# Attention and a SoLU layer on one core: the softmax scale moved into the turn of the exponentials, with another order of work and of loads

## The chip, the core and the metric

The kernel runs on one core of a Trainium2 chip. The metric is the device time of one execution in microseconds; lower is better. A kernel is timed in several runs, and one further execution is profiled. Five engines work side by side: TensorE (PE in the profile, its weight loads PEld), VectorE (DVE), ScalarE (ACT), GpSimd (POOL) and SyncE (SP), which here only issues loads.

## The reference

Local attention with block summaries, over 4 batches, 8 heads, 768 positions, head size 64; then a feed-forward layer with the SoLU activation. Cut to what matters:

```python
k_sum = k.reshape(B, H, nb, block, D).max(axis=3)       # 24 blocks of 32
v_sum = v.reshape(B, H, nb, block, D).mean(axis=3)
scores_l = where(|i - j| < 16, scale * q @ k.T, -1e9)
scores_s = scale * q @ k_sum.T + log(block)
a = exp(scores_all - max);  a = a / (sum(a) + 1e-9)     # over [scores_l, scores_s]
x = a @ concat(v, v_sum)                                # then (3072, 512)
h = x @ w_in                                            # (3072, 1024)
solu = h * softmax(h)
ln = (solu - mean) / sqrt(var + 1e-6) * g_ln
out = ln @ w_out                                        # (3072, 512)
```

All inputs are float32, q and k larger than the others by a factor of 8.

## The kernel before, in words

**Attention** goes in 24 steps `(b, g, pp)`: batch, a group of 4 tiles of 64 queries, and a half of the four head pairs. A step has 8 blocks of 128 rows (two tiles of 64 queries) by 120 columns: 96 neighbouring keys and 24 block maxima. `scores` gathers the keys into `kw`, multiplies on TensorE into `s` (a PSUM buffer), and on VectorE adds the mask and takes the row maximum into `nm` while it copies to `e` (L574). ScalarE takes the exponentials of `e` in place and their sums `z` (L582). VectorE takes 1 / `z` and multiplies `e` by it (`MUL_E`, listed by its helper at L265). `values_turn` turns the result: 16 transposes of 64x120 with the identity into `t` (a PSUM buffer, L610), copied to `at` in two halves by ScalarE (L258) or VectorE (L259). `values` multiplies `at` with the values `vt`, whose last 24 rows are the block means `vsum`, into `x` (L649), which is split into a high and a low part, `xh` and `xl`.

**The layer** goes in 24 tiles of 128 tokens, one for each attention step. `first(t)`: three products for each piece of w_in (high and low parts) into `h` (L674, 24 products of 512 columns), row maxima `hm`, exponentials `he`, the SoLU product, centring, squares, and a small chain on GpSimd for the inverse root `y`. `turn(t)`: 16 transposes into `lt`, split into `lh` and `ll`. `second(t)`: 24 products with w_out into `o` (L752), scaled by `y` and stored from ScalarE's queue.

**Weights.** w_in and w_out come as 64-bit words in 16 pieces of 512 KB (`raw`). For each piece `rounded` and `split_w_in` or `split_w_out` do eight operations on VectorE, ScalarE or GpSimd (`cv`, then `w`): w_in's eight pieces before the first `h`, w_out's two at a time in the first four tiles.

**Block means.** For batch 0 and 1 they are products with a selector (`vs_ps<-st_v`), later a tree of additions on GpSimd (`st_v`, `vacc`, L478) and products with the identity (L493). `load_v2` writes `vsum` into `vt` by a DMA on ScalarE's queue (L518).

**What sets the order.** The program isn't issued as it is written. `Plan` collects operations, each with the engines that may run it, the planner's price there, and what it depends on. `issue` simulates the engines with those prices, always takes the operation that can begin first (ties by a due time that is the place of its TensorE user in the program), chooses the engine by price plus a surcharge (`DEAR`), and then issues everything in the simulated order, each engine's queue in strict order. `keep_up` puts products with a tile of zeros (`zero`, L877; "idle products" below) into gaps of the first 80 us that the simulation sees on TensorE. The first loads follow the string `LOADS`: k, q are keys and queries of the first step, w pieces of w_in, r value rows for the means, v and V the first two `vt`, Q the second group's queries. From tile `NEAR` = 6 on, the TensorE work of a step is tied into one run: `t`, `lt`, `x`, `s`, then `o` and `h`.

Of the kernel before, what the change touches and what calls it, by code (L numbers as in the profile page):

```python
# [10 lines left out]
F32 = mybir.dt.float32  # L11
# [21 lines left out]
KC = WIN + NB  # L33
# [7 lines left out]
MEANS = 2  # L41
DIRECT = 0
NEAR = 6
WPT = 2


LOADS = "kqkkqkwwwwwwwwrrrvQV"
NEG = -8.0e9
# [24 lines left out]
class Plan:  # L73
# [65 lines left out]
    def issue(self):  # L139
        ready, free, then, dma, held = {}, {}, {}, 0.0, 0.0  # L140
        for o in self.ops:
            o.left = len(o.deps)
            for d in o.deps:
                d.users.append(o)
        for o in reversed(self.ops):
            o.due = min([u.due for u in o.users] + ([o.prio] if "pe" in o.can else []), default=o.prio)
            if "sp" in o.can:
                o.due = o.prio

        def enter(o):  # L150
# [38 lines left out]
        order = []  # L189
        while len(order) < len(self.ops):  # L190
            t, e, o = min(((x[0], e, x[1]) for e in ready for x in [take(e)] if x),
                          key=lambda x: (x[0], x[2].due))
# [18 lines left out]
        at, done = self.START, set()  # L211
        for o in order:
            if o.engine == "pe":
                while at + self.SYNC < min(o.start, self.FILL):
                    at += self.keep_up(at, done)
                at = max(at, o.start) + o.cost * (2 if o.start < self.COLD else 1)
            done.add(o)
            o.fn()

# [12 lines left out]
def attn_then_solu(ctx: ExitStack, tc: tile.TileContext, q, k, v, vr, vb, w_in, w_out, g_ln, out):  # L232
# [3 lines left out]
    nc = tc.nc  # L236
    plan = Plan()
    op = plan.op
# [9 lines left out]
    ADD_W = ((dve, 0.62), (pool, 1.46))  # L248
    MUL_E = ((pool, 1.8), (dve, 1.07))

# [24 lines left out]
    g_sb = const.tile([P, NFC], F32, name="g_sb")  # L275
    zero = const.tile([P, 512], BF16, name="zero")

    make_identity(nc, ident)
    nc.gpsimd.memset(mhalf, -0.5)
    nc.vector.memset(zero, 0.0)  # L280
# [50 lines left out]
    def load_w(key, src, after=()):  # L331
        raw[key] = x = plan.buf(const, [P, 1024], I32, f"w{key}", 1, f"raw{key}")
        op(sp, 0.43, lambda: nc.sync.dma_start(out=x.ap, in_=src.bitcast(I32)), w=[x], nbytes=P * 4096,
           after=after)

    def rounded(key, tag, bufs):

# [4 lines left out]
        high, low = (lambda: st.ap[:, 0]), (lambda: st.ap[:, 1])  # L342


        op(act, 0.57, lambda: nc.scalar.activation(
            out=high().bitcast(F32), in_=words(1).bitcast(F32), func=AF.Copy, scale=2.0 ** -112),
            r=[x], w=[(st, 0)], alt=[(dve, 0.34, lambda: nc.vector.tensor_scalar(
                out=high().bitcast(F32), in0=words(1).bitcast(F32), scalar1=2.0 ** -112, scalar2=None,
                op0=ALU.mult))], port=True)

# [164 lines left out]
    def load_v2(b, g):  # L515
        x, y = vt[b, g], vsum[b]

        return op(act, 0.8, lambda: nc.scalar.dma_start(  # L518
            out=x.ap[WIN:KC], in_=y.ap[WIN:KC, :].rearrange("p (o c) -> p o c", o=1).broadcast_to([NB, G, DM])),
                  r=[y], w=[(x, 1)], nbytes=NB * 8192)  # L520

    def scores(b, g, pp, direct=False, each=False):
# [89 lines left out]
    def values_turn(b, g, pp):  # L612
        nm_ = f"{b}_{g}_{pp}"
        e = es.pop((b, g, pp))
# [200 lines left out]
    for t in range(NT):  # L815
# [3 lines left out]
        if not near:  # L819
            run(scores(*step(t + 2), t < DIRECT))  # L820

# [99 lines left out]
```

## Time and profile before

| | |
|---|---|
| median of three runs | 406.12 us (405.17 to 410.25) |
| the profiled execution's own time | 406.69 us |
| its span, first to last instruction | 404.9 us |
| TensorE busy | 388.3 us, 3702 matmul records |
| VectorE, ScalarE, GpSimd busy | 300.5, 230.5, 88.8 us |
| granted clock of TensorE, mean | 0.99 |
| read from HBM, written | 40.11 MB, 6.29 MB |

How to read the rows: a group row gives line, engine, operation, what is written from what, partitions by elements, count, then busy time in us and mean ns of one, then the engine's idle time just before such instructions and what ended most of it. A row of the timeline begins with its start and its length in us, from the span's start; a bracket at its end is the idle time before it and who ended it. Matmul records are pipelined, so what a group costs TensorE is the distance from its first start to the next group's first start, not the sum of its lengths. PEld is the load of the stationary operand, ACTq and SPq a queue's issue of a DMA.

### The profile page before, as it was taken

Reading aid. Unit: us, or ns where it says so; the run is one execution under the profiler, and the core shown is the slowest. Engines: PE = TensorE matmul, PEld = TensorE weight load, DVE = VectorE, ACT = ScalarE, POOL = GpSimd, SP = SyncE. Lnnn points to the kernel's source line nnn. Section 1 sums busy time; section 2 is a strip of 40 time slices with the busy share of each in tenths; the row PEclk is TensorE's granted clock in tenths of the full one; section 3 lists DMA queues with packets and bytes.
Section 4 is the critical chain, followed back from the end, with each engine's and each line's share of the span. In section 5 each row is a group of like instructions: output and inputs, shape, how many; then the busy total and the mean of one; then the engine's idle time right before and its main releaser. Section 6 shows DMA issues by size and latency. Waiting matters only on the chain.

```text
span 404.9 us, 9684 instructions
## 1 busy us (share of the span) xinstructions
PE 388.3 (96%) x3702; PEld 299.6 (74%) x3702; DVE 300.5 (74%) x933; ACT 230.5 (57%) x711; POOL 88.8 (22%) x231
## 2 busy tenths in 40 slices
PE   7999999986988999998999999999999999999996
PEld 3436667664876788887888888878878888888776
DVE  4998999989887886776877777687678766654430
ACT  2967788963898664565455664646545453423311
POOL 3020240305581412216202211201201221011100
PEclk9999999996999999999999999999999999999999
DMA  8999992044257040044350040141130000000011
GB/s 270 411 409 364 404 336 75 25 123 152 86 186 258 26 159 28 28 176 126 108 182 21 28 182 2 40 169 42 41 137 2 28 28 26 2 26 28 26 53 52
DMA packets 14994, 49.24 MB, mean 122 GB/s; under 512 B 1836, under 2 KB 2092, under 8 KB 13412
## 3 DMA queue, kind: packets, MB, share of 16 engines
q1 hardware_dynamic: 10112, 40.12, 27.4%
q10 hardware_dynamic: 4836, 8.51, 6.9%
q8 instruction: 29, 0.48, 0.5%
q14 instruction: 17, 0.14, 0.1%
HBM read 40.11 MB, written 6.29 MB: 115 GB/s over the span
## 4 chain that ended last, share of the span: by engine, by line
PE 71%; DMA 12%; DVE 11%; ACT 3%; issue 1%; POOL 1%; SPq 0%; ACTq 0%; POOLq 0%
PE o L752 32%; PE h L674 23%; PE x L649 5%; PE s L555 4%; DMA kraw<-in_k 3%; DMA qt<-in_q 3%; PE lt L610 3%; DMA raw<-in_w_in 2%; PE t L610 2%; DMA vt<-in_v 2%; DMA st_v<-in_vb 1%; DVE e L265 1%; DVE e L574 1%; DVE hm L684 1%; DVE ksum L416 1%
## 5 line engine op out<-in xcount | busy, mean ns | idle before, releaser
L752 PE MATMUL o<-w,lh 128*128 128x512 f32 (+1 forms) x400 | 129.6, 393 | 4.8 <-DVE w L379 4.8
L674 PE MATMUL h<-w,xh 128*128 128x512 f32 x384 | 125.6, 396 | 0.0
L582 ACT ACTIVATE e<-e,nm 128x120 f32<-128x120 f32 x192 | 73.1, 385 | 40.2 <-DVE nm L574 31.1
L752 PEld LDWEIGHTS o<-w,lh 128*128 128x128 f32 x400 | 74.6, 189 | 23.9 <-DVE w L379 5.6
L674 PEld LDWEIGHTS h<-w,xh 128*128 128x128 f32 x384 | 72.1, 188 | 17.4 <-DVE he L697 0.5
L752 PE MATMUL o<-w,ll 128*128 128x512 f32 (+1 forms) x200 | 77.3, 386 | 0.0
L674 PE MATMUL h<-w,xl 128*128 128x512 f32 x192 | 75.5, 393 | 0.0
L684 DVE TENSOR_REDUCE hm<-h 128x1 f32<-128x512 f32 x48 | 32.7, 684 | 33.8 <-PE h L674 33.5
L716 POOL TENSOR_SCALAR ss<-ss 128x1 f32<-128x1 f32 x24 | 6.4, 268 | 167.7 <-ACT sq L712 151.9
L752 PEld LDWEIGHTS o<-w,ll 128*128 128x128 f32 x200 | 38.0, 190 | 6.4
L674 PEld LDWEIGHTS h<-w,xl 128*128 128x128 f32 x192 | 36.1, 188 | 7.8 <-DVE xl L655 0.3
L574 DVE CUSTOM_DVE_ANT_0 e<-s,mask 128x120 f32<-128x120 f32 x192 | 40.6, 276 | 0.1
L689 ACT ACTIVATE he<-h,hm 128x512 f32<-128x512 f32 x48 | 32.8, 691 | 13.9 <-DVE hm L686 13.9
L258 ACT COPY at<-t 120x512 f32<-120x512 f32 x29 | 16.3, 585 | 35.6 <-PE t L610 35.1
L582 ACT ACTIVATION_READ_ACCUMULATOR e<-e,nm 128x1 f32 x192 | 36.4, 190 | 0.0
L697 DVE SCALAR_TENSOR_TENSOR he<-h,hz,he 128x512 f32<-128x512 f32 x48 | 34.2, 744 | 0.2
L737 DVE TENSOR_TENSOR ll<-lt,lh 128x512 fp32r<-128x512 f32 x48 | 31.6, 679 | 0.2
L649 PE MATMUL x<-at,vt 120*64 120x64 f32 (+1 forms) x768 | 28.3, 225 | 0.4 <-DVE at L259 0.4
L265 DVE TENSOR_TENSOR e<-e,z 128x960 f32<-128x960 f32 x24 | 28.5, 1189 | 0.1
L478 POOL TENSOR_TENSOR st_v<-st_v 96x512 f32<-96x512 f32 (+3 forms) x28 | 22.1, 791 | 29.2 <-DMA st_v<-in_vb 28.5
L649 PEld LDWEIGHTS x<-at,vt 120*64 120x64 f32 (+1 forms) x768 | 24.6, 138 | 5.2 <-issue 2.3
L712 ACT ACTIVATE sq<-he 128x1024 bf16<-128x1024 f32 x24 | 25.2, 1050 | 5.3 <-DVE hm L684 2.7
(93 smaller groups left out, 504.2 us busy)
## 6 DMA issues: line engine op xcount, KB each, us to landing
vt<-in_v SPq DMA_DIRECT2D x12, 1024.0 KB, 6.2
kraw<-in_k SPq DMA_DIRECT2D x16, 400.0 KB, 8.5
out<-os ACTq DMA_DIRECT2D x23, 256.0 KB, 2.1
qt<-in_q SPq DMA_DIRECT2D x11, 512.0 KB, 5.4
raw<-in_w_in SPq DMA_DIRECT2D x8, 512.0 KB, 10.1
raw<-in_w_out SPq DMA_DIRECT2D x8, 512.0 KB, 10.1
st_v<-in_vr SPq DMA_DIRECT2D x6, 512.0 KB
st_v<-in_vb SPq DMA_DIRECT2D x8, 384.0 KB, 3.4
```

The lines of the kernel that those rows point to most:

```text
L265: by = {dve: lambda: nc.vector.tensor_tensor(out=to(), in0=a(), in1=b(), op=kind), pool: lambda: nc.gpsimd.tensor_tensor(out=to(), in0=a() ...
L478: op(pool, 0.15 + w * 0.0021, lambda w=w, o=o: nc.gpsimd.tensor_tensor(out=o.ap[:n, :w], in0=x.ap[:n, :w], in1=x.ap[:n, w:2 * w], op=ALU.add),
L574: nc.vector.tensor_tensor_reduce(out=e.ap[:, n, :], in0=sc.ap[:, j, (2 * i + up) * KC:(2 * i + up + 1) * KC], in1=mask[:, mi, :], scale=-S ...
L582: nc.scalar.activation(out=e.ap[:, n, :], in_=e.ap[:, n, :], func=AF.Exp, bias=nm.ap[:, n:n + 1], scale=-1.0, accum_out=z.ap[:, n:n + 1])
L649: nc.tensor.matmul(xp()[j * D:(j + 1) * D, i, qs], vs.ap[:k, u, cs], at.ap[:k, u % 2, n[j] + u // 2, :], start=not apart, stop=not apart o ...
L674: nc.tensor.matmul(hp.ap, a.ap[:, c, ts], w.ap[:, i], start=(c == 0 and n == 0), stop=(c == NKC - 1 and n == 2))
L684: op(dve, 0.6, lambda i=i, hp=hp: nc.vector.tensor_reduce(out=nms.ap[:, i:i + 1], in_=hp.ap, op=ALU.max, axis=AX.X, negate=True), r=[hp], ...
L689: op(act, 0.71, lambda i=i, hp=hp: nc.scalar.activation(out=part(i), in_=hp.ap, func=AF.Exp, bias=nm.ap, accum_out=zs.ap[:, i:i + 1]), r=[ ...
L697: op(dve, 0.67, lambda i=i, hp=hp: nc.vector.scalar_tensor_tensor(out=part(i), in0=hp.ap, scalar=zs.ap[:, 0:1], in1=part(i), op0=ALU.mult, ...
L712: op(act, 1.13, lambda: nc.scalar.activation(out=sq.ap, in_=e.ap, func=AF.Square, accum_out=ss.ap), r=[e], w=[sq, ss])
L737: op(dve, 0.6, lambda part=part, r=r: nc.vector.tensor_tensor(out=part(lo), in0=tp.ap[:, r], in1=part(hi).bitcast(F32), op=ALU.subtract), ...
L752: nc.tensor.matmul(o.ap[:, cols], a.ap[:, f, :], w.ap[:, i, cols], start=(f == 0 and n == 0), stop=(f == NFC - 1 and n == 2))
```

## The change

1. The multiplication of the exponentials (128x960) goes. Instead `ident2`, two 64x64 identities one above the other, is multiplied by 1 / `z` into `dg` (128x512, `MUL_Z`): eight pairs of diagonal 64x64 blocks. `values_turn` multiplies `e` with these blocks by 16 ordinary float32 products where it had 16 transposes; the planner's price of the group stays 0.82.
2. `issue` tries 64 orders. In the first the due times are as before, in the others they carry noise (3.0 in standard deviation, in places of the program). Of the orders that come to an end, the one whose last TensorE operation ends first by the planner's prices is issued. The simulation itself moves to `order`.
3. Other prices: VectorE's surcharge is 1.0 for 0.6; a DMA behind 50 us is taken to land 2.0 us after its transfer, not 0.6.
4. The first loads come in another order; `load_v2` of batches 1 to 3 goes on SyncE's queue, of batch 0 stays on ScalarE's. `DIRECT`, which was 0, and `rebias`, a part of `rounded` with a name of its own, change nothing by themselves.

```diff
-LOADS = "kqkkqkwwwwwwwwrrrvQV"
+LOADS = "wkwqkkwkqwwrwrrwwvQV"
...
+    LATE = 50.0
...
-    DEAR = {"dve": 0.6, "act": 0.3, "pool": 1.0}
+    DEAR = {"dve": 1.0, "act": 0.3, "pool": 1.0}
+    TRIES, NOISE = 64, 3.0
...
+        due, best = [o.due for o in self.ops], None
+        for seed in range(self.TRIES):
+            noise = random.Random(seed)
+            for o, x in zip(self.ops, due):
+                o.due = x + (noise.gauss(0.0, self.NOISE) if seed else 0.0)
+            order = self.order()
+            if order:
+                end = max(o.end for o in order if "pe" in o.can)
+                if best is None or end < best[0]:
+                    best = end, order, [(o.start, o.end, o.engine, o.cost, o.fn) for o in self.ops]
...
-                o.end = dma + 0.6
+                o.end = dma + (0.6 if dma < self.LATE else 2.0)
...
-    MUL_E = ((pool, 1.8), (dve, 1.07))
+    MUL_Z = ((pool, 1.37), (dve, 0.6))
...
+    nc.gpsimd.tensor_tensor(out=ident2, in0=ident[:, :QT], in1=ident[:, QT:], op=ALU.add)
...
-        return op(act, 0.8, lambda: nc.scalar.dma_start(
+        e, cost, queue = (sp, 0.43, nc.sync) if b else (act, 0.8, nc.scalar)
+        return op(e, cost, lambda: queue.dma_start(
...
-        tt(MUL_E, ALU.mult, lambda: e.ap, lambda: e.ap,
-           lambda: z.ap.rearrange("p (u o) -> p u o", o=1).broadcast_to([P, 8, KC]), r=[z], w=[e], port=True)
-        es[b, g, pp] = e
+        dg = plan.buf(sb, [P, 8, QT], F32, "dg", 2, "dg" + nm_)
+        tt(MUL_Z, ALU.mult, lambda: dg.ap, lambda: ident2[:].rearrange("p (o q) -> p o q", o=1).broadcast_to([P, 8, QT]),
+           lambda: z.ap.rearrange("p (u o) -> p u o", o=1).broadcast_to([P, 8, QT]), r=[z], w=[dg], port=True)
+        es[b, g, pp] = e, dg
...
-        yield 0.82, lambda: turn_halves(tp.ap[:KC], lambda n: e.ap[:, n, :]), [e], [tp]
+        def mm():
+            for n in range(8):
+                for r in range(2):
+                    rows = slice(r * QT, (r + 1) * QT)
+                    nc.tensor.matmul(tp.ap[:KC, r, n, :], e.ap[rows, n, :], dg.ap[rows, n, :], start=True, stop=True)
+        yield 0.82, mm, [e, dg], [tp]
```

Counted over the whole order: VectorE loses 24 multiplications of `e`, 16 copies of `at`, 15 centrings of `he`, 7 scalings of `os` and 3 products of low parts of w_in, and gets 23 of `dg`; ScalarE gets the 16 copies, 7 scalings and 3 centrings and loses 9 issues of `vt<-vsum`; GpSimd gets 12 centrings, those 3 products and one `dg`; TensorE has 74 idle products for 82.

TensorE in the steady part, one period, before:

```order
L674 MATMUL h11_1_2751<-w7_546,xh1_2_2253 128x512
L610 MATMUL t2_1_0_2770<-ident_66,e2_1_0_2694 120x64 x16
L610 MATMUL lt8_2790<-ident_66,he8_2228 128x64 x16
L649 MATMUL x2_0_1_2807<-at2_0_1_2628,vt2_0_2066 64x64 x16
L555 MATMUL s2_1_1_2835<-kw2_1_1_2453,qt2_1_2077 64x120 x16
L752 MATMUL o7_2860<-w8_718,lh7_2660 128x512
```

and now:

```order
L711 MATMUL h11_1_2746<-w7_551,xh1_2_2262 128x512
L653 MATMUL t2_1_0_2780<-dg2_1_0_2763,e2_1_0_2702 120x64 x16
L641 MATMUL lt8_2800<-ident_66,he8_2235 128x64 x16
L686 MATMUL x2_0_1_2817<-at2_0_1_2639,vt2_0_2065 64x64 x16
L584 MATMUL s2_1_1_2844<-kw2_1_1_2461,qt2_1_2078 64x120 x16
L789 MATMUL o7_2870<-w8_723,lh7_2665 128x512
```

The sequence of the groups is the same; the first group's second operand is `dg` where it was the identity, its count the same.

ScalarE where w_out's last pieces (`w14`, `w15`; `raw15` is the last as it comes) are made ready, before:

```order
L377 ACTIVATE w13_1260<-cv13_1121,g_sb_69 128x512
L587 ACTIVATE z1_0_0_1179<-z1_0_0_1179 128x8
L258 CAST lh1_1262<-lt1_1212 128x8x64
L518 DMA vt1_1_1229<-vsum1_896 24x4x512
L345 ACTIVATE cv15_1280<-raw15_272 128x512
L377 ACTIVATE w14_1291<-cv14_1254,g_sb_69 128x512
```

and now:

```order
L380 ACTIVATE cv15_1266<-raw15_267 128x512
L611 ACTIVATE e1_0_0_1177,z1_0_0_1213<-e1_0_0_1177,nm1_0_0_1178 128x120 x4
L281 CAST lh1_1286<-lt1_1218 128x8x64
L616 ACTIVATE z1_0_0_1213<-z1_0_0_1213 128x8
L406 ACTIVATE w14_1299<-cv14_1251,g_sb_69 128x512
L406 ACTIVATE w15_1307<-cv15_1266,g_sb_69 128x512
```

The DMA `vt1_1<-vsum1` is gone from this queue (it stands on SyncE's now, behind the load of `vt1_1`), and the first operation on `raw15` stands earlier.

SyncE's loads from the first value rows (`st_v0_0`) to the two first `vt`, before:

```order
L424 DMA st_v0_0_153<-in_vr 128x1024
L424 DMA st_v0_1_158<-in_vr 128x1024
L424 DMA st_v0_2_160<-in_vr 128x1024
L512 DMA vt0_0_179<-in_v 128x2048
L506 DMA qt0_1_183<-in_q 128x1024
L512 DMA vt0_1_185<-in_v 128x2048
```

and now:

```order
L453 DMA st_v0_0_124<-in_vr 128x1024
L453 DMA st_v0_1_127<-in_vr 128x1024
L358 DMA raw6_131<-in_w_in 128x1024
L358 DMA raw7_133<-in_w_in 128x1024
L815 DMA g_sb_69<-in_g_ln 128x8
L535 DMA qt0_1_137<-in_q 128x1024
L453 DMA st_v0_2_143<-in_vr 128x1024
L541 DMA vt0_1_147<-in_v 128x2048
L541 DMA vt0_0_151<-in_v 128x2048
```

The first two `st_v` now stand ahead of w_in's last two pieces, the third behind them, and the two `vt` have changed places.

More of the change, by code (lines that the diff above doesn't have):

```diff
@@ L1 @@
 import math
+import random
 from contextlib import ExitStack
@@ L139, in issue @@
     def issue(self):
-        ready, free, then, dma, held = {}, {}, {}, 0.0, 0.0
         for o in self.ops:
-            o.left = len(o.deps)
             for d in o.deps:
@@ L148, in issue, with order @@
                 o.due = o.prio
+        due, best = [o.due for o in self.ops], None
[8 more added lines that the diff above has]
+                    best = end, order, [(o.start, o.end, o.engine, o.cost, o.fn) for o in self.ops]
+        _, order, kept = best
+        for o, x in zip(self.ops, kept):
+            o.start, o.end, o.engine, o.cost, o.fn = x
+        at, done = self.START, set()
+        for o in order:
+            if o.engine == "pe":
+                while at + self.SYNC < min(o.start, self.FILL):
+                    at += self.keep_up(at, done)
+                at = max(at, o.start) + o.cost * (2 if o.start < self.COLD else 1)
+            done.add(o)
+            o.fn()
+    def order(self):
+        ready, free, then, dma, held = {}, {}, {}, 0.0, 0.0
+        for o in self.ops:
+            o.left = len(o.deps)
         def enter(o):
@@ L191, in issue @@
             t, e, o = min(((x[0], e, x[1]) for e in ready for x in [take(e)] if x),
-                          key=lambda x: (x[0], x[2].due))
+                          key=lambda x: (x[0], x[2].due), default=(0.0, None, None))
+            if o is None:
+                return None
             for f in o.can:
@@ L210, in issue @@
                     enter(u)
[L211 to L218, printed above, removed]
+        return order
     def keep_up(self, at, done):
@@ L276, in attn_then_solu @@
     zero = const.tile([P, 512], BF16, name="zero")
+    ident2 = const.tile([P, QT], F32, name="ident2")
     make_identity(nc, ident)
+    nc.gpsimd.tensor_tensor(out=ident2, in0=ident[:, :QT], in1=ident[:, QT:], op=ALU.add)
     nc.gpsimd.memset(mhalf, -0.5)
@@ L334, in load_w, with rebias @@
            after=after)
+    def rebias(x, words, st, i):
+        to = lambda: st.ap[:, i].bitcast(F32)
+        op(act, 0.57, lambda: nc.scalar.activation(
+            out=to(), in_=words(1).bitcast(F32), func=AF.Copy, scale=2.0 ** -112),
+            r=[x], w=[(st, i)], alt=[(dve, 0.34, lambda: nc.vector.tensor_scalar(
+                out=to(), in0=words(1).bitcast(F32), scalar1=2.0 ** -112, scalar2=None,
+                op0=ALU.mult))], port=True)
     def rounded(key, tag, bufs):
@@ L342, in rounded @@
         high, low = (lambda: st.ap[:, 0]), (lambda: st.ap[:, 1])
[L345 to L349, printed above, removed]
+        rebias(x, words, st, 0)
         op(act, 0.57, lambda: nc.scalar.activation(
@@ L516, in load_v2 @@
         x, y = vt[b, g], vsum[b]
[L518 removed]
+        e, cost, queue = (sp, 0.43, nc.sync) if b else (act, 0.8, nc.scalar)
+        return op(e, cost, lambda: queue.dma_start(
             out=x.ap[WIN:KC], in_=y.ap[WIN:KC, :].rearrange("p (o c) -> p o c", o=1).broadcast_to([NB, G, DM])),
[L520 removed]
+            r=[y], w=[(x, 1)], nbytes=NB * 8192)
     def scores(b, g, pp, direct=False, each=False):
@@ L613, in values_turn @@
         nm_ = f"{b}_{g}_{pp}"
-        e = es.pop((b, g, pp))
+        e, dg = es.pop((b, g, pp))
         tp = plan.buf(ps, [P, 2, 8, QT], F32, "s", 2, f"t{nm_}")
-        yield 0.82, lambda: turn_halves(tp.ap[:KC], lambda n: e.ap[:, n, :]), [e], [tp]
+        def mm():
[4 more added lines that the diff above has]
+        yield 0.82, mm, [e, dg], [tp]
         at = plan.buf(sb, [P, 2, 8, QT], F32, "at", 2, f"at{nm_}")
@@ L819, in attn_then_solu @@
         if not near:
-            run(scores(*step(t + 2), t < DIRECT))
+            run(scores(*step(t + 2)))
         if t == NEAR - 1 or (near and j == 0 and n + 3 < len(its)):
```

1 line of the change is left out of this document (removed).

## The prediction

> **What bounds the kernel now.** I read the page's sums first, then busy time by stretch, then TensorE's own order of time inside the stretches, and last what the other engines did where TensorE waited.
>
> ```profile
> PE 388.3 (96%) x3702; PEld 299.6 (74%) x3702; DVE 300.5 (74%) x933; ACT 230.5 (57%) x711; POOL 88.8 (22%) x231
> PEclk9999999996999999999999999999999999999999
> ```
>
> TensorE is busy for 96% of the span, and its granted clock drops once, in the tenth slice. The stretches:
>
> ```profile
> core 0: us, PE busy (x) PEld busy (x) DVE busy (x) ACT busy (x) POOL busy (x), PEclk, DMA share, GB/s
> 0.00:36.30 36.30, 32.33 (x348) 15.36 (x348) 29.32 (x82) 23.53 (x62) 7.11 (x29) 1.00 0.96 368
> 36.30:87.80 51.50, 50.83 (x522) 36.62 (x519) 50.77 (x174) 42.68 (x139) 10.57 (x19) 1.00 0.60 212
> 87.80:101.50 13.70, 8.95 (x68) 6.01 (x67) 11.58 (x34) 4.75 (x7) 5.62 (x7) 0.75 0.44 129
> 101.50:141.70 40.20, 37.48 (x391) 29.92 (x389) 33.52 (x108) 32.66 (x108) 20.45 (x49) 1.00 0.41 139
> 141.70:333.70 192.00, 190.61 (x1936) 155.95 (x1935) 142.94 (x470) 105.87 (x354) 39.05 (x105) 1.00 0.25 80
> ```
>
> Three regimes. Up to 36.3 us the loads set the pace (DMA share 0.96). From 36.3 to 101.5 us VectorE has no room (50.77 of 51.50 us), and from 87.8 to 101.5 us TensorE waits for it: 8.95 of 13.70 us busy. From 141.7 us on TensorE is full, VectorE at 74%, ScalarE at 55%, so there every added microsecond of TensorE work lengthens the kernel, and VectorE time saved buys nothing. One period there, TensorE alone:
>
> ```profile
> 201.29 0.69 PE L610 MATMUL t<-ident,e 64*120 64x64 f32 x16
> 201.81 0.67 PE L610 MATMUL lt<-ident,he 64*128 64x64 f32 x16
> 202.41 1.15 PE L649 MATMUL x<-at,vt 120*64 120x64 f32 x32
> 203.49 1.05 PE L555 MATMUL s<-kw,qt 64*64 64x120 f32 x32
> 204.47 0.50 PE L752 MATMUL o<-w,lh 128*128 128x512 f32 x1
> ```
>
> What a group costs is the distance to the next group's start: `t` 0.52 us, `lt` 0.60, `x` 1.08, `s` 0.98. And the counts matter: the program issues 16 transposes for `t` and the trace has 16 records; it issues 16 float32 products for `x`, 16 for `s`, and the trace has 32 each. A float32 product is two passes here, a transpose is one.
>
> **The change, part by part.**
>
> *The products in place of the transposes.* The order shows 24 groups of 16 turn instructions, now `t<-dg,e` with the same shapes. They become float32 products, so 32 records. Price of a record: `x` has products with 64 moving columns, two at a time side by side, 1.08 us / 32 = 34 ns; the transposes, with the same 64x120 stationary tile, two halves of the rows at a time, ran 0.52 / 16 = 33 ns, so the weights of such a pair load in that time. Both say 33 to 34 ns: 1.08 us for a group. Bounds: from below, two passes with nothing else would still be no cheaper than the 0.52 us seen for one. From above, products that don't run in pairs:
>
> ```profile
> L493 PE MATMUL vs_ps<-vacc,ident 96*24 96x64 f32 x32 | 2.1, 220 | 0.0
> L265 DVE TENSOR_TENSOR e<-e,z 128x960 f32<-128x960 f32 x24 | 28.5, 1189 | 0.1
> L265 DVE TENSOR_TENSOR w<-cv,w 128x512 fp32r<-128x512 f32 x8 | 5.4, 700 | 0.9 <-ACT w L258 0.9
> L266 POOL TENSOR_TENSOR cv<-cv 128x512 int32<-128x512 int32 x3 | 4.3, 1436 | 2.3 <-DVE cv L360 2.3
> L705 POOL TENSOR_SCALAR he<-he,nmu 128x512 f32<-128x512 f32 x1 | 1.7, 1701 | 6.0 <-DVE nmu L700 6.0
> L877 PE MATMUL vs_ps<-zero 128*128 128x512 bf16 x53 | 13.9, 417 | 1.2 <-DVE zero L280 1.2
> ```
>
> These have 64 moving columns too and took 2.1 us / 32 = 66 ns, 2.1 us a group. I take 1.08, since the operands come in two row halves as the transposes' did. About 15 of the groups stand ahead of `lt` as above (+0.56 each); 7 more stand among other groups, where a transpose group took 0.61 us (100.84 to 101.45, below), +0.47 each; the first two lie ahead of the first `h` and are counted in the start. 15 x 0.56 + 7 x 0.47 = **+11.7 us**, with nothing to hide it.
>
> The Trainium skill has rules against this edit. "Perfetto Trace Analysis", section Transposes, asks that a logical transpose be a transpose and not an ordinary matmul; "TensorE: Matmul & The Clock Gate", section Terms, calls the transpose mode 4x faster for FP32. By that a group would take 4 x 0.52 = 2.1 us, and the sum would be 22 us higher than mine; the trace's two records, not four, and `x` at 1.08 us speak for a factor of two.
>
> *Scaling leaves VectorE.* Out go 24 multiplications of the exponentials (1189 ns each, 28.5 us). In come 23 of 128x512 on VectorE, the nearest row `w<-cv,w` at 0.70, 16 us, and one on GpSimd at about 1.4. Copies of `at` go from 19 to 3 on VectorE, centring of `he` from 36 to 21. ScalarE gets 16 of those copies, GpSimd 12 more centrings at 1.70 us where VectorE took under 0.5. After 141.7 us this is worth nothing; before 101.5 us it is what TensorE waits for.
>
> *The wait at 88 us.* TensorE, then VectorE, then ScalarE:
>
> ```profile
> 87.85 0.39 PE L752 MATMUL o<-w,lh 128*128 128x512 f32 x1
> 88.08 0.39 PE L752 MATMUL o<-w,ll 128*128 128x512 f32 x1
> ...
> 91.98 0.49 PE L752 MATMUL o<-w,lh 128*128 128x512 f32 x1 [2.57 <-DVE w L379]
> ...
> 95.12 0.80 PE L752 MATMUL o<-w,lh 128*128 128x512 f32 x1 [2.18 <-DVE w L379]
> ...
> 96.70 1.88 PE L555 MATMUL s<-kw,qt 64*64 64x120 f32 x32
> 98.51 0.80 PE L752 MATMUL o<-w,lh 128*128 128x512 f32 x1
> ...
> 100.84 0.69 PE L610 MATMUL t<-ident,e 64*120 64x64 f32 x16
> 101.45 0.50 PE L752 MATMUL o<-w,lh 128*128 128x512 f32 x1
> ```
>
> ```profile
> 89.91 0.69 DVE L356 SCALAR_TENSOR_TENSOR cv<-cv 128x512 int32<-128x512 int32 x1 [1.98 <-ACT cv L345]
> ...
> 94.31 0.75 DVE L379 SCALAR_TENSOR_TENSOR w<-cv,g_sb,w 128x512 fp32r<-128x512 f32 x1
> ```
>
> ```profile
> 88.33 0.84 ACTq L518 DMA_DIRECT2D vt<-vsum  x1
> 89.21 0.66 ACT L345 ACTIVATE cv<-raw 128x512 f32<-128x512 f32 x1 [3.11 <-DMA vt<-in_v]
> ```
>
> Twelve products of the first `o` take 8.85 us (87.85 to 96.70) where 12 x 0.23 = 2.8 would do: they wait for the last pieces of w_out, which VectorE finishes at 95.1. It was itself held 1.98 us by ScalarE, whose queue stood for 3.11 us at the issue of `vt<-vsum`, until `vt<-in_v` had landed. Behind the wait the clock is down: `s` takes 1.81 us in place of 0.98, six `o` 2.33 in place of 1.4. In all 6.0 + 0.8 + 0.9 = 7.8 us (rounded sums). In the changed order this `vt<-vsum` is on SyncE's queue, where only loads for later tiles stand behind it; and of VectorE's work up to the last piece six multiplications (7.1 us) become six of 0.7 (4.2), three products of low parts (2.1) go to GpSimd and three copies of `at` (2.1) to ScalarE; against that two more casts, a copy and one 0.7 us addition. Net about -5 us, and -2 for the wait: 95.1 becomes about 88.5. TensorE gets there near 90: it stood at this place at 89.4, starts 0.7 later, has four dearer groups ahead of it (1.9) and 2.1 less idle work. I take 1.0 us as left: **-6.8 us**. Bounds: 0 (the wait moves on to another engine) and -7.8.
>
> *Copies of `at` and `s`.* TensorE waited in these places, the rows with both parts of a wait:
>
> ```profile
> 115.72 1.03 PE L649 MATMUL x<-at,vt 120*64 120x64 f32 x28 [0.39 <-DVE at L259]
> 117.43 1.05 PE L555 MATMUL s<-kw,qt 64*64 64x120 f32 x32 [0.67 <-DVE hz L692]
> 131.68 1.05 PE L555 MATMUL s<-kw,qt 64*64 64x120 f32 x32 [1.29 <-issue]
> ```
>
> The second and third stand behind the second copy of `at` on VectorE, late behind other work there. Both copies are now on ScalarE nearly everywhere: **-2.4 us**, bounds 0 and -2.4.
>
> *Idle products.* Behind the first `h` the order has 9 of the products with `zero` where it had 18; they start 0.23 us apart when the clock is full: **-2.1 us** at most; if they only filled waits, 0.
>
> *The start.* Weights now load between keys and queries, and the first `vt` last.
>
> ```profile
> 22.23 5.31 PE L436 MATMUL vs_ps<-st_v,sel 128*24 128x512 f32 x12 [0.30 <-DMA st_v<-in_vr]
> ...
> 28.51 1.05 PE L555 MATMUL s<-kw,qt 64*64 64x120 f32 x32 [0.43 <-DMA qt<-in_q]
> 29.49 0.65 PE L641 MATMUL x<-at,vsum 24*64 24x256 f32 x4
> ...
> 31.88 0.39 PE L877 MATMUL h<-zero 128*128 128x512 bf16 x1
> ```
>
> By the sizes of the loads, 6720 KB had landed at 22.2 us and 9280 KB at 28.5: 408 KB a us. In the new order the second `st_v` is complete at 6208 KB, 21.0 us, and `vt0_0` at 10304 KB, 31.0. TensorE's order then is: four products of `vs_ps` (0.88 each, the first two as soon as 5696 KB are there, all done at 23.2), `t` 1.08, 7 idle 1.6, `s` 0.98, two more `vs_ps` 1.75, `t` 1.08, `s` 0.98, 4 idle 0.9: 31.6 us, just past the landing of `vt0_0`; two groups of `x` at 2.4 (29.49 to 31.88) and 7 idle: the first `h` at 38.0 us, against 36.3. One `s` (0.98) that stood behind it is then done: **+0.7 us**, bounds -1 and +4.
>
> *Sum.* 11.7 - 6.8 - 2.4 - 2.1 + 0.7 = +1.1 us on the profiled span of 404.9, so 406.0. That execution's own time is 406.69, the median of the three runs 406.12 (405.17 to 410.25): I forecast the median at 406.12 + 1.1 = **407 us**, no change that counts. A measurement of this kernel tells about 2% from no change, that is under 398 or over 414.
>
> **The rivals.**
>
> *The products cost what the transposes did* (0.15). If both passes of a pair hide in the weight loads, +11.7 falls away: 407 - 12 = 395 us, faster. For it: a transpose group is bound by something other than its 64 columns, since `lt`, with 128 stationary columns, is slower than `t`, with 120. Against it: two records each, and `x` pays for its second.
>
> *The halves don't run side by side* (0.07). Then a group takes the 2.1 us of the row L493 and 22 groups cost 22 x 1.0 more: 429 us, slower. It decides above 1.4 us a group (407 + 22 x 0.33 = 414). The rule of the skill gives the same 2.1. Against it: the transposes ran in pairs on the same halves.
>
> *The wait at 88 us stays* (0.09). GpSimd, with centrings at 1.70 us, takes work for w_out (1.44 each) and holds buffers; w_out's last piece stays at 95 us and the copies win nothing: 407 + 6.8 + 2.4 = 416, slower. It decides when the last piece is later than about 95. For it: GpSimd's operations are two to three times as long as VectorE's, and the 64 orders are judged with the group of products at the transposes' price. Against it: of w_out's chain only two rounding additions are GpSimd's now, and three were before.
>
> *More is won* (0.12). All waits before 141.7 us go and a group takes 0.9: 407 - 1 - 4 = 402, still no change. *The start slips by 5 us* (0.05), because the first transposes wait for `st_v`: 412, no change.
>
> **How the numbers follow.** Forecast 0.52 (its own range 402 to 412). Faster 0.15 from the first rival; slower 0.07 + 0.09 = 0.16; within 2% the other 0.69. The range of 8 in 10 takes in the third rival and reaches to the first: 395 to 416.
>
> **What would show it.** Right: 32 records to a group of `t`, 1.05 to 1.15 us from its start to that of `lt`; a period 0.5 us longer behind 141.7 us; no wait of `o` for w_out over 1 us, and no lowered clock near 95 us; the first `h` at 37 to 39 us. Wrong: a group under 0.8 us or over 1.4; TensorE waiting for `w` again; new waits of `s` or `x` in each period, which would mean that the copies on ScalarE come too late.

## The result and the profile after

The changed kernel takes 422.69 us (median of 4 runs, 422.61 to 422.76), the kernel before in the same comparison 406.52: 1.038 times as long, interval 1.031 to 1.045. It is slower; 407 was forecast, 395 to 416 as the range. The profiled execution has a span of 421.0 us; 404.9 before, 406.0 by the sum of the prediction. So 15.0 us of the span are to be explained.

From the page of the changed kernel: the sums, TensorE's clock by slice, and the chain that ended last.

```profile
PE 414.5 (98%) x4078; PEld 325.8 (77%) x4078; DVE 268.0 (64%) x892; ACT 244.7 (58%) x736; POOL 99.1 (24%) x248
PEclk9999999999999999999999999999999999999999
PE 95%; DMA 4%; SPq 0%; ACT 0%; issue 0%
```

VectorE has 32 us less work, TensorE 26 us more, the clock no longer drops, and the chain is TensorE nearly alone. The stretches of the changed kernel say how far that goes (length, then busy us of PE, PEld, DVE, ACT, POOL, then clock, DMA share, GB/s):

```profile
0.00:39.39 39.39, 36.08 (x413) 18.51 (x413) 31.04 (x106) 26.55 (x78) 12.66 (x36) 1.00 0.96 365
39.39:88.00 48.61, 48.61 (x529) 36.92 (x526) 44.31 (x143) 37.09 (x112) 9.12 (x19) 1.00 0.53 189
88.00:102.00 14.00, 14.00 (x153) 11.30 (x152) 12.62 (x44) 13.11 (x39) 9.09 (x11) 1.00 0.53 171
102.00:142.00 40.00, 40.00 (x437) 32.79 (x437) 30.73 (x101) 28.11 (x91) 21.11 (x50) 1.00 0.45 142
142.00:334.00 192.00, 192.00 (x1980) 158.55 (x1978) 113.12 (x408) 107.68 (x346) 38.54 (x103) 1.00 0.24 79
```

From the first `h` at 39.39 us on, TensorE waits for nothing up to its last product. Every wait that the prediction wanted gone is gone, and the kernel is slower all the same. The reason stands in one period, TensorE alone:

```profile
203.67 1.90 PE L653 MATMUL t<-dg,e 64*120 64x64 f32 x32
205.40 0.67 PE L641 MATMUL lt<-ident,he 64*128 64x64 f32 x16
205.99 1.15 PE L686 MATMUL x<-at,vt 120*64 120x64 f32 x32
207.07 1.05 PE L584 MATMUL s<-kw,qt 64*64 64x120 f32 x32
208.06 0.50 PE L789 MATMUL o<-w,lh 128*128 128x512 f32 x1
```

From start to start, `lt` (0.59), `x` (1.08) and `s` (0.99) cost what they did. `t` costs 1.73 us where the transposes took 0.52 and where 1.08 was forecast: 32 records, as forecast, of 54 ns and not 34. In the 15 groups that stand right ahead of `lt` it is 1.73, in the other nine 1.82 or 1.83 (57 ns).

The weight loads (mean ns of one behind the busy time), first before, with those of `x` and `o` beside `t`, then now:

```profile
L752 PEld LDWEIGHTS o<-w,lh 128*128 128x128 f32 x400 | 74.6, 189 | 23.9 <-DVE w L379 5.6
L649 PEld LDWEIGHTS x<-at,vt 120*64 120x64 f32 (+1 forms) x768 | 24.6, 138 | 5.2 <-issue 2.3
L610 PEld LDWEIGHTS t<-ident,e 64*120 64x120 f32 x384 | 13.3, 135 | 10.0 <-issue 8.2 <-ACT e L582 0.7 <-ACT he L689 0.4
```

```profile
L653 PEld LDWEIGHTS t<-dg,e 64*120 64x120 f32 x768 | 42.2, 181 | 9.5 <-issue 7.4
L653 PE MATMUL t<-dg,e 64*120 64x64 f32 x768 | 45.5, 268 | 0.0
L789 PE MATMUL o<-w,lh 128*128 128x512 f32 (+1 forms) x400 | 128.6, 391 | 0.0
L281 ACT COPY at<-t 120x512 f32<-120x512 f32 x45 | 24.3, 589 | 75.1 <-PE t L653 74.2
L742 POOL TENSOR_SCALAR he<-he,nmu 128x512 f32<-128x512 f32 x13 | 15.4, 1188 | 74.2 <-DVE nmu L737 74.2
```

There are twice as many loads of `t`, and each is 46 ns longer for the same 64x120 tile. That is the first trace of the cause; the experiments below settle it. The row of `o` shows no idle time of TensorE ahead of any of its 400 products. ScalarE has 45 of the 48 copies of `at`, and GpSimd 13 centrings of `he`, as the order said, these at 1.19 us and not at the 1.70 of the prediction. The place that was the wait at 88 us before:

```profile
94.07 1.90 PE L653 MATMUL t<-dg,e 64*120 64x64 f32 x32
95.90 0.50 PE L789 MATMUL o<-w,lh 128*128 128x512 f32 x1
...
96.80 1.05 PE L584 MATMUL s<-kw,qt 64*64 64x120 f32 x32
97.78 1.15 PE L686 MATMUL x<-at,vt 120*64 120x64 f32 x32
98.86 0.71 PE L641 MATMUL lt<-ident,he 64*128 64x64 f32 x16
99.50 0.50 PE L789 MATMUL o<-w,lh 128*128 128x512 f32 x1
```

No bracket of idle time, and `s` takes 0.98 us in place of 1.81, at full clock.

### The profile page after: what moved, and what is told of

Read it like the earlier page. It is cut to its first block, busy times and chain, and to the rows that moved or that the text cites. A ratio compares the mean times of both kernels' runs of the same rounds, so it can differ in the third digit from the quotient of the medians.

```text
span 421.0 us, 10428 instructions
## 1 busy us (share of the span) xinstructions
PE 414.5 (98%) x4078; PEld 325.8 (77%) x4078; DVE 268.0 (64%) x892; ACT 244.7 (58%) x736; POOL 99.1 (24%) x248
## 4 chain that ended last, share of the span: by engine, by line
PE 95%; DMA 4%; SPq 0%; ACT 0%; issue 0%
PE o L789 33%; PE h L711 33%; PE t L653 10%; PE x L686 6%; PE s L584 5%; PE lt L641 3%; DMA st_v<-in_vr 3%; DMA qt<-in_q 1%; PE vs_ps L465 1%; PE x L914 1%; PE h L914 1%; PE x L678 1%; PE vs_ps L522 0%; PE vs_ps L478 0%; SPq L436 0%; ACT os L794 0%
## 5 line engine op out<-in xcount | busy, mean ns | idle before, releaser
L711 PE MATMUL h<-w,xh 128*128 128x512 f32 x384 | 127.8, 399 | 0.0
L281 ACT COPY at<-t 120x512 f32<-120x512 f32 x45 | 24.3, 589 | 75.1 <-PE t L653 74.2
L653 PEld LDWEIGHTS t<-dg,e 64*120 64x120 f32 x768 | 42.2, 181 | 9.5 <-issue 7.4
L653 PE MATMUL t<-dg,e 64*120 64x64 f32 x768 | 45.5, 268 | 0.0
L742 POOL TENSOR_SCALAR he<-he,nmu 128x512 f32<-128x512 f32 x13 | 15.4, 1188 | 74.2 <-DVE nmu L737 74.2
L282 DVE CAST lh<-lt 128x512 fp32r<-128x512 f32 x17 | 11.7, 690 | 28.9 <-ACT lh L281 17.4
L281 ACT CAST lh<-lt 128x512 fp32r<-128x512 f32 x31 | 17.7, 594 | 18.0 <-PE lt L641 9.0
## 6 DMA issues: line engine op xcount, KB each, us to landing
raw<-in_w_out SPq DMA_DIRECT2D x8, 512.0 KB, 12.1
```

The source lines that it names most:

```text
L281: by = {act: lambda: nc.scalar.copy(out=to(), in_=of()), dve: lambda: nc.vector.tensor_copy(out=to(), in_=of()), pool: lambda: nc.gpsimd.t ...
L653: nc.tensor.matmul(tp.ap[:KC, r, n, :], e.ap[rows, n, :], dg.ap[rows, n, :], start=True, stop=True)
L711: nc.tensor.matmul(hp.ap, a.ap[:, c, ts], w.ap[:, i], start=(c == 0 and n == 0), stop=(c == NKC - 1 and n == 2))
```

## The experiments

The kernel before took 406.4 to 406.8 us (medians of 7 runs) beside the twelve runs below.

**What a group of products is bound by.** Five kernels change one thing each in how the turn is done. Each was timed once, and what is read from them is what a group costs in its trace.

*Eight products of the upper row half, then eight of the lower* (`halves_apart`):

```diff
-            for n in range(8):
-                for r in range(2):
+            for r in range(2):
+                for n in range(8):
```

> The changed kernel with the 16 products of t in another order: the eight of the upper half of the rows, then the eight of the lower half, so that neighbours never lie in different halves. Theory A (load, then stream; only different halves overlap): a record 98 ns and a little, a group 3.2 to 3.5 us, span about 458. Theory B (loads queue anyway, streams are hidden behind the next load): unchanged, 1.7 to 1.8. Theory C (streams queue anyway): unchanged, 1.7 to 1.8, span 421.

457.02 us, span 455.3. A group among other work, and what comes behind it:

```profile
121.01 3.21 PE L653 MATMUL t<-dg,e 64*120 64x64 f32 x32
124.14 0.80 PE L711 MATMUL h<-w,xh 128*128 128x512 f32 x1
```

3.13 us, 98 ns a record on average, against 57 with the halves in turn. By the starts of the single records it is 105 ns from one record to the next of the same half; the average is lower because the first records of the lower half run beside the last of the upper. So the halves did run side by side in the changed kernel, and something that takes 105 ns a record queues within a half. Theory A's number nearly came (3.2 to 3.5), but from this run alone it can't be said what queues: the loads or the streams. The `h` behind the group takes 0.80 us because the granted clock is at half for 3.4 us from 124.2 us on, though TensorE waited for nothing; why it fell was not tried.

*Half of the moving columns* (`moving32`):

```diff
-... tp.ap[:KC, r, n, :], e.ap[rows, n, :], dg.ap[rows, n, :] ...
+... tp.ap[:KC, r, n, :32], e.ap[rows, n, :], dg.ap[rows, n, :32] ...
```

> The changed kernel with only the first 32 of the 64 moving columns in each product of t; the copies to at read these 32 twice, so half of the turned values are left out. From the profile before: float32 records of 24 stationary columns take 437 ns with 512 moving columns and 63 with 64, so 0.835 ns a moving column (53 ns for 64) and 9 ns for 24 stationary columns (45 for 120). Theory A (in each half of the rows a record loads its weights, then streams; the two halves overlap): a record of the changed kernel is (45 + 53) / 2 and a little, measured 54; now (45 + 27) / 2 and the same little, 41, a group 1.3 us. Theory B (the loads of both halves queue, streams are hidden): a group stays at 1.73. Theory C (the streams of both halves queue, 53 each): a group falls to 1.05, where the transposes' 33 ns a record would end it. Each 0.1 us of a group is 2.4 us of the kernel: A 411, B 421, C 405 us of span.

422.6 us, span 420.9:

```profile
203.53 1.87 PE L653 MATMUL t<-dg,e 64*120 64x32 f32 x32
205.23 0.70 PE L641 MATMUL lt<-ident,he 64*128 64x64 f32 x16
```

1.70 us for 1.73, and inside the group 105 ns for a pair of records, one of each half, as in the changed kernel. The streams can be halved without a gain: what queues is not the streams. Theory B's number; those of A and C fall.

*64 stationary columns of 120* (`stat64`), and later *96* (`stat96`, written with 96 for 64), in all but the first two steps, with the copies of `at` and the products `x` cut to the same rows:

```diff
-... tp.ap[:KC, r, n, :], e.ap[rows, n, :], dg.ap[rows, n, :] ...
+... tp.ap[:kc, r, n, :], e.ap[rows, n, :kc], dg.ap[rows, n, :] ...      # kc = 64
```

> The changed kernel with only the first 64 of the 120 stationary columns in the products of t, in all but the first two steps, and with x over those 64 rows; the other key columns are left out there. Theory A (load, then stream, halves overlap): a record (24 + 53) / 2 and a little, 43, a group 1.35 to 1.4 us. Theory B (loads of both halves queue): 27 to 34 a record, as x has with 64 stationary columns, a group 0.9 to 1.1. Theory C (streams of both halves queue): 53 to 54 a record, the group stays at 1.73. Span: A 412, B 406, C 421 us.

> The changed kernel with 96 of the 120 key columns as stationary columns in the products of t, and products of x over 96 rows, in all steps but the first two; the other key columns (the block maxima) are left out of the result. Theory D (the group is bound by loading its stationary columns, 64 columns 34 ns a record, 120 columns 54): on the line between, 45 ns a record, a group of 1.45 us, span 421.0 - 22 x 0.3 = 414 to 415. Rival (a step: a tile of more than 64 columns takes both column halves of the array and cannot share it): 54 ns a record as with 120, span 420 to 421. Rival that everything in this group stands on the number of output rows in other ways: below 40 ns a record.

`stat64`: 405.2 us, span 403.5. `stat96`: 415.86 us, span 414.1. A group of each:

```profile
208.68 1.15 PE L655 MATMUL t<-dg,e 64*64 64x64 f32 x32
209.75 0.71 PE L641 MATMUL lt<-ident,he 64*128 64x64 f32 x16
```

```profile
200.00 1.57 PE L655 MATMUL t<-dg,e 64*96 64x64 f32 x32
201.41 0.67 PE L641 MATMUL lt<-ident,he 64*128 64x64 f32 x16
```

1.07 us with 64 columns, 1.41 with 96, 1.73 with 120: a group grows by the stationary column, and there is no step behind 64 columns. A group's average, 67, 88 and 108 ns for a pair of records, takes in its longer first pair and its end. By the starts of the single records, a pair inside the group takes 58, 85 and 105 ns: 0.83 ns for each column and 5 ns beside. Each of the three theories of the first expectations misses at least one of these runs. What fits them all is theory D: the loads of the stationary columns set the pace, they queue within a row half, and two halves load side by side. The number of output rows, which the stationary columns set too, is not what does it: the transposes write the same 120 rows, at 65 ns a pair on a group's average (0.52 us / 8). With 64 columns a group costs exactly what I forecast, because the row I forecast it from, `x`, has 64 stationary columns. (The span of `stat64` falls by 17.5 us, more than its 22 groups give, 14.9, because `x` is cut too: `x` and `s` together take 1.90 us for 2.07.)

*Transposes, halves apart* (`t_halves_apart`): the changed kernel with transposes and the scaling of the exponentials restored, and the two loops of `turn_halves` exchanged as above, which turns `lt` too.

> The changed kernel with the transposes and the scaling of the exponentials restored, and every group of transposes (t and lt) issued as eight of the upper row half, then eight of the lower. Theory D (loads of one row half queue, loads of two halves overlap, and a transpose's load of 120 columns takes 65 ns where a product's takes 108): 65 ns a record in t and 74 in lt, 1.04 and 1.18 us a group, span 396.7 + 24 x 1.1 = 423, 419 to 425. Rival (transposes are bound by something else than loads, so that the order of the halves doesn't matter to them): 396 to 398.

408.46 us, span 406.7: between the two.

```profile
118.82 0.97 PE L638 MATMUL t<-ident,e 64*120 64x64 f32 x16
119.72 0.50 PE L781 MATMUL o<-w,lh 128*128 128x512 f32 x1
```

Transposes queue in a half as well: 0.90 us a group, 0.61 with the halves in turn. From one record to the next of the same half it is 59 ns, and a pair takes 59 ns with the halves in turn; for `lt`, with 128 stationary columns and the same 64 moving ones, it is 62 to 63. The 65 of the expectation was a group's average, with its longer first pair. In the steady part the lower half of `t` runs beside the upper half of `lt`, as their interleaved records show, so that both together grow from 1.11 to 1.53 us and not by 1.1. That is 0.42 us in each of 15 places, and 0.3 for each of the nine groups of either kind that stand alone: 11.7 us, of which the span shows 10.0. Mechanism confirmed, both numbers wrong.

Together: a pair of halves costs one load, 105 ns for products and 59 for transposes of 120 columns, and the streams of 64 columns hide under it. The lengths of the weight loads say the same: 135 ns on average with 64 stationary columns (`stat64`), 161 with 96 (`stat96`) and 181 with 120, but 135 for the transposes' 120. Why a transpose loads the same tile faster, no run shows. The Trainium skill, "TensorE: Matmul & The Clock Gate", section LDWEIGHTS, says that a load takes its columns / 1.2 ns whatever its rows. As an estimate that would be 53, 80 and 100 ns for 64, 96 and 120 columns, and the products' 58, 85 and 105 agree but for the same 5 ns. The transposes' 59 for 120 columns do not, and here the measurement decides. The Trainium skill, same page, Part 3 (Packing small matmuls), lets loads overlap running products only where the row groups differ. The halves of `t` agree: 105 ns for one record in one half, 105 for two in two. `x` does not: its products share their 120 rows and differ in the column half, and a pair of them takes 58 ns as well.

**What the rest of the change is worth.**

*The change without the products* (`t_new_order`): transposes and scaling as before; the new loads, prices, queue and 64 orders stay.

```diff
-        tt(MUL_Z, ALU.mult, lambda: dg.ap, ...
+        tt(MUL_E, ALU.mult, lambda: e.ap, lambda: e.ap, ...
...
-        yield 0.82, mm, [e, dg], [tp]
+        yield 0.82, lambda: turn_halves(tp.ap[:KC], lambda n: e.ap[:, n, :]), [e], [tp]
```

> The changed kernel with the multiplication of the exponentials and the 16 transposes of before put back; the 64 orders, the prices, the loads and the SyncE queue stay as changed. Theory (the products cost it all): a group of t falls from 1.73 to 1.83 us back to 0.52 to 0.62, 24 groups give back 28.5 us; VectorE gets 12 us of work back, and of the waits that the change removed up to 6 us may return: span 393 to 399, time 394 to 401, faster than before by 2 to 3%. Rival (the new order and loads gain nothing by themselves, the waits went because VectorE was relieved): the wait near 90 us returns, 403 to 408, the same as before.

398.24 us (397.8 to 398.98), 0.980 of the kernel before, interval 0.976 to 0.983: clearly shorter than both kernels, though against the kernel before it is just about the 2% from which a change is told. Its sums, and the waits that are left near 88 us:

```profile
PE 385.3 (97%) x3690; PEld 296.9 (75%) x3690; DVE 275.5 (69%) x882; ACT 246.0 (62%) x741; POOL 116.5 (29%) x252
```

```profile
87.41 0.69 PE L638 MATMUL t<-ident,e 64*120 64x64 f32 x16 [0.54 <-DVE e L288]
88.78 0.34 PE L678 MATMUL x<-at,vt 120*64 120x64 f32 x4 [0.68 <-ACT at L281]
...
93.00 0.50 PE L781 MATMUL o<-w,lh 128*128 128x512 f32 x1 [0.17 <-DVE w L406]
...
94.74 0.50 PE L781 MATMUL o<-w,lh 128*128 128x512 f32 x1 [0.78 <-ACT os L786]
```

With the scaling back on VectorE the wait for `w` is 0.17 us; VectorE still has 25 us less to do than in the kernel before, since the new order gives GpSimd 28 and ScalarE 16 us more. So the wait for `w` goes without the change of the turn; some 2 us of other waits are left here.

*The products alone* (`products_old_order`): the kernel before with `dg` and the 16 products, nothing else.

> The kernel before with the products alone: the diagonal blocks and the 16 products a group, with the old order rules, the old loads and the old queue for the block means. A group of products costs 1.73 to 1.83 us where a transpose group cost 0.52 to 0.62, so 24 groups add 1.21 x 24 = 29 us to TensorE's work. Theory 1 (additive: the scaling off VectorE wins about 5 us, as the changed kernel with and without it says, and the rest of the gain of the change, 8 us, is the order's and not here): span 404.9 + 29 - 5 = 429, 427 to 431. Theory 2 (the dearer groups fall into the waits of TensorE before 142 us, some 14 us in the kernel before, so that products cover for them): span 418 to 424, as the changed kernel.

425.62 us, 1.050 of the kernel before, interval 1.044 to 1.056; span 423.4. Theory 2: the products' 24 x 1.21 = 29 us lengthen the span by 18.5, so some 10.5 us went elsewhere. TensorE's idle time falls by 7.1 us (404.9 - 388.3 = 16.6 before, 423.4 - 413.9 = 9.5 now), and the lowered clock is gone, which had cost 3.4 us (0.75 in 13.70 us). What of this went because VectorE had less to do, and what because TensorE came later, isn't told apart. At the old place TensorE still waits, for less:

```profile
94.37 0.50 PE L760 MATMUL o<-w,lh 128*128 128x512 f32 x1 [0.97 <-DVE w L381]
...
95.67 1.05 PE L557 MATMUL s<-kw,qt 64*64 64x120 f32 x32 [0.33 <-DVE ll L745]
97.78 1.89 PE L624 MATMUL t<-dg,e 64*120 64x64 f32 x32 [1.06 <-DVE dg L265]
```

The four spans make a square: 404.9 and 423.4 with the old order, 396.7 and 421.0 with the new one. The new order wins 8.2 us with transposes and 2.4 with products. Of the 8.2 us, 5.2 are idle time of TensorE (16.6 to 11.4) and 3.0 busy time (388.3 to 385.3), nearly what the lowered clock had cost. The products cover most of what the order removes.

**Where the order's 8 us come from.** Each of the next runs undoes one part in `t_new_order`, except `a_one_order`, which does so in the changed kernel. An edit of this kind makes the planner write another order throughout, so that a microsecond either way says little.

*One order in place of 64*, `TRIES` = 1, with transposes (`t_one_order`) and in the changed kernel (`a_one_order`):

> The changed kernel with transposes and scaling restored (398.24 us, span 396.7) and only the first of the 64 orders, the one without noise. Theory (the search finds the gain: the planner's first order leaves waits of TensorE that another avoids): 401 to 405 us. Rival (the other prices, the queue of the block means and the order of loads make the gain, the noise nothing): 397 to 400 us.

> The changed kernel with products (422.69 us), and only the first of the 64 orders, which is another than the one that was chosen. Theory (TensorE has no idle time left in the changed kernel and its work is the same in every order, so that an order can only add waits and idle products): 422 to 426 us. Rival (the choice is made at a wrong price of the product group, and the first order is better on the chip): 417 to 421 us.

398.34 us (398.0 to 399.86): with transposes the first of the 64 orders is the one that the search chooses, and every engine's instructions are the same, so that this is the same program again. The search found nothing there, and my theory fell. In the changed kernel it does choose another: 423.45 us (423.3 to 423.88) without it for 422.69, within the range given. The theory's way there was not quite so: TensorE's work is not the same in both (412.0 us busy for 414.5, with 66 idle products for 74), and its idle time is 3.1 us more. A difference of 0.8 us is too small to say that the search won it.

*The old loads* (`t_old_loads`): `LOADS` as before.

> The changed kernel with transposes and scaling restored (398.24 us, span 396.7; its first h began at 34.0 us, 36.3 in the kernel before), and the old order of the first loads. Theory L (the new order of loads starts the layer earlier, and that stays): first h at about 36.3, 400 to 402 us. Rival (the start is lost again at the wait near 88 us, which the other engines set): 397.5 to 399 us.

401.54 us (400.68 to 403.09), 0.988 of the kernel before, interval 0.985 to 0.991. Theory L's number, with a miss in it: the first `h` begins at 35.15 us, only 1.1 later than with the new loads; more is lost between 36 and 88 us, where TensorE is busy for 47.1 of 52 us (50.5 with the new ones). At 98.5 us a product of `o` waits for `w` again, 1.4 us.

*ScalarE's queue for the block means* (`t_queue_act`):

```diff
-        e, cost, queue = (sp, 0.43, nc.sync) if b else (act, 0.8, nc.scalar)
+        e, cost, queue = act, 0.8, nc.scalar
```

> The changed kernel with transposes and scaling restored (398.24 us), and all copies of the block means back on ScalarE's queue. Theory Q, the prediction's (ScalarE's stand at that issue holds up the last pieces of w_out, and TensorE's wait at 88 us with them): products of the first o wait again, 3 to 5 us, 401 to 404 us. Rival (the stand is hidden behind work that goes to other engines): 397.5 to 399.5 us, and no wait of o longer than in the kernel with the new queue.

398.16 us (397.1 to 400.45): nothing, and no product of `o` waits for `w`. With the other parts of the change in place, the queue, to which the prediction gave 2 us of the earlier end of w_out, is not what ended the wait; with the old prices and loads it wasn't tried.

*The old prices* (`t_old_prices`):

```diff
-    DEAR = {"dve": 1.0, "act": 0.3, "pool": 1.0}
+    DEAR = {"dve": 0.6, "act": 0.3, "pool": 1.0}
...
-                o.end = dma + (0.6 if dma < self.LATE else 2.0)
+                o.end = dma + 0.6
```

> The changed kernel with transposes and scaling restored (398.24 us) and the planner's old prices: surcharge of VectorE 0.6 and landing of a DMA 0.6 us after its transfer. With the new ones VectorE had 275.5 us of work, before 300.5. Theory P (the surcharge moves work from VectorE to GpSimd and ScalarE, and that removes the waits of TensorE before 102 us): VectorE back near 300 us, 402 to 405 us. Rival (VectorE's sum doesn't matter as long as w_out's pieces come in time): 397 to 400 us.

405.63 us (403.88 to 406.73), 0.997 of the kernel before, interval 0.994 to 1.001. Nearly the whole gain is gone, and the time is 0.6 us above theory P's range:

```profile
PE 390.9 (97%) x3693; PEld 299.5 (74%) x3698; DVE 293.3 (73%) x916; ACT 237.7 (59%) x721; POOL 90.3 (22%) x238
```

```profile
94.53 1.50 PE L678 MATMUL x<-at,vt 120*64 120x64 f32 x32 [2.00 <-ACT at L281]
96.49 0.80 PE L781 MATMUL o<-w,lh 128*128 128x512 f32 x1 [0.46 <-DVE w L406]
```

VectorE has 18 us of work back and GpSimd 26 less, as theory P says. The waits of TensorE don't come back as a sum: its idle time is 12.1 us, 11.4 in `t_new_order`. But two of them are long, 1.83 us at 67.6 us and 2.00 at 94.5, both for the copies of `at`, where the longest behind the first `h` was 0.9; and the granted clock is down behind both. Its mean is 0.97 from 36 to 88 us and 0.88 from 88 to 102, 1.00 in `t_new_order`, which makes some 3 us of the 5.6 by which TensorE's busy time grows. So the prices make most of the gain, partly by the clock; the rest of the way is open. Which of the two prices does it, the surcharge or the DMA's landing, wasn't tried.

## Why the prediction was wrong, point by point

- **The price of a product group: the step that failed.** "Both say 33 to 34 ns: 1.08 us for a group." Neither row could say it. `x` has 64 stationary columns and these products have 120 (1.07 us with 64, shown by `stat64`); the transposes have the 120 columns, but their loads are quicker (59 ns for 105), so "the weights of such a pair load in that time" held for transposes only. Measured: 1.73 to 1.83. For 22 groups that is 15 x 0.65 + 7 x 0.74 = 14.9 us, and two more stand before the first `h`: 2 x 0.75 = 1.5. This one term makes 16.4 us of miss where 15.0 came; the others, by subtraction, came out 1.4 better than forecast.
- **Two passes, 32 records:** right, and so was that the two halves run side by side. The rival in which they don't had the wrong mechanism and the nearer price (2.1 where 1.73 came); its threshold of 1.4 us a group, from which the kernel is slower, was passed. The rule of the Trainium skill, "TensorE: Matmul & The Clock Gate", section Terms, pointed the right way; the factor is 1.73 / 0.52 = 3.3 here, not 4.
- **Bounds:** 0.52 and 2.1 held the price, but the range of the time reached only to the lower end (395) and not to the upper (429, put at 0.07). The rows that would have said more were the weight loads in the profile before, with their columns, not the pace of another group: 138 ns for the 64 columns of `x`, 189 for the 128 of `o`, and 135 for the transposes' 120. On the line between the first two, a product's load of 120 columns is some 183 ns, 48 longer than the transposes'. A pair of transposes took 65 ns (0.52 us / 8), so 16 pairs of products would take about 16 x (65 + 48) ns = 1.8 us: an estimate from rows that were there, near the 1.73 to 1.83 that came.
- **The wait at 88 us, -6.8:** it went altogether (-7.8 was the bound). The cause was mis-told. The queue of the block means, put back alone, changes nothing (`t_queue_act`), and the scaling's move isn't needed for it (`t_new_order`). The old loads bring back 1.4 us of the wait for `w` (`t_old_loads`), and the planner's old prices, which the prediction gave no term, two long waits for `at` with a lowered clock (`t_old_prices`). VectorE had no room only up to 87.8 us, not to 101.5: in the last stretch it was busy for 11.58 of 13.70 us.
- **Copies of `at` and `s`, -2.4, and idle products, -2.1:** the copies' waits are gone, and 9 idle products are behind the first `h`, as forecast.
- **The start, +0.7:** the first `h` at 39.39 us for 38.0: the two dear groups (1.5) account for it. The 6720 and 9280 KB that the prediction says had landed are each some 0.6 to 0.7 MB low (by the DMA packets 7437 KB at 22.23 us, 9913 at 28.51); in its times this nearly cancels.
- **From 141.7 us on saved VectorE time buys nothing:** right: TensorE is busy for 192.00 of 192.00 us there, and it now has no wait from 39 us on.

## What to carry to other kernels

Price a small product by its own stationary tile: its columns set the load, the load sets the pace when few columns stream, and a transpose with the same tile is no measure for it. When one part of a change removes work from an engine that is waited for and another adds work to the engine that waits, build each alone: here the new order was worth 8 us and the turn by products cost 24 more, and only the square of four kernels says so. Look at a planner's prices before its search: undoing two changed numbers cost 7 us, undoing 64 noisy orders under one.

## What the runs showed of the hardware that was not expected

- A float32 product with 64 rows and 120 stationary columns loads in 105 ns, a float32 transpose with the same tile in 59 ns (`halves_apart`, `t_halves_apart`). For products it is 58, 85 and 105 ns with 64, 96 and 120 columns (`stat64`, `stat96`, the changed kernel).
- Loads into the two row halves overlap wholly, also with this length: a pair takes 105 ns for products and 59 for transposes, no more than one load. A group has some 50 ns more in its first pair.
- With 64 moving columns the stream costs nothing beside such a load: with 32 columns in place of 64 a pair takes 105 ns as before, and a group 1.70 us for 1.73.
- The granted clock can fall without a wait of TensorE: in `halves_apart` it is twice at half for 3.4 us, from 124.2 and from 226.6 us on, each time directly behind a group of `t`, while TensorE waits for nothing behind the first `h`.
